# Row maximum in a spare PSUM column, read there by two one-column operations

## The chip, the cores and the metric

The kernel runs on one core of a Trainium2 chip, as one program from the load of the inputs to the last store. The metric is device time in microseconds. Inside the core five engines take their own instructions in order: PE (TensorE, matrix multiplication), DVE (VectorE), ACT (ScalarE), POOL (GpSimd) and SP (SyncE, which here only issues DMAs). PE writes into PSUM, eight banks of 512 fp32 columns by 128 partitions; DVE and ACT read and write PSUM and SBUF; POOL works on SBUF here.

## The reference, cut to what matters

Attention over 8 batches and 8 heads with a sequence of 576 and head dimension 64, where each row keeps only the scores within `tau` of its maximum, and then a mixture-of-experts layer over the 4608 resulting rows of 512:

```python
scores = scale * np.matmul(q, k.transpose(0, 1, 3, 2))     # scale = 1/8
thresh = np.max(scores, axis=-1, keepdims=True) - tau
scores = np.where(scores >= thresh, scores, -1000000000.0)
scores = scores - np.max(scores, axis=-1, keepdims=True)
attn = np.exp(scores)
attn = attn / (np.sum(attn, axis=-1, keepdims=True) + 1e-09)
attn_out = np.matmul(attn, v)
...
# MoE: rows with x @ w_skip > 0 go to the expert of the largest logit:
h = np.maximum(xc[mask] @ w1[e], 0.0)
y[mask] = gate_w[mask, None] * (h @ w2[e])
```

## The kernel before, in words

The attention works on 32 groups; a group `g` is two heads of one batch. Each group has nine items `i`: for each of four blocks of 128 query rows one item for either head, and a last item (`M`) that holds the 64 left-over rows of both heads. So there are 288 items, each a tile of 128 query rows by 576 keys. `plan_item` (L669) registers the steps of one item:

- `score` (L686, PE): two fp32 products of 288 columns, into two PSUM banks, of which columns 0 to 287 are used (`HS` is 288). A ring of three such pairs (`sps`, `SPB = 3`) is shared by the items; a pair is freed when the item's `mask` is done.
- `top` (L691, DVE): the maximum of the raw scores over both banks, into column 0 of the item's four columns of the SBUF tile `mx`.
- `small` (L695, DVE): one SCALAR_TENSOR_TENSOR on two columns, `mx[1:3] = cd[0:2] * mx[0] + cd[2:4]`. With the constant tile `cd` (1, -0.125, -8 tau, 0), built at the start (L400 to L404), it makes the threshold in column 1 and the bias of the exponential in column 2. Both of its tensor inputs, and its output, lie in SBUF.
- `expo` (L700, ACT): `exp(0.125 * score + bias)` from PSUM into the SBUF tile `p`.
- `mask` (L706, DVE): `(score >= threshold) * p`, from PSUM and SBUF into `p`.

After every second item, and after the ninth, `fph` (L510 on ACT, L512 on DVE) makes the f16 high part `pk` of `p`, `fpl` (L737, POOL) the f16 low part, and `turn` (L748 and L743, issued on SP) transposes them by DMA into `pt` or `ptm`. `plan_av` (L768) multiplies them with the values on PE (L788, L792); ACT takes the result out of PSUM, POOL scales it (L841, L854), and PE computes the router's logits (L923). The values themselves are split in two f16 parts by ACT and POOL (L645).

The order of all this on the engines is not written out. `Plan` (L138) is a list scheduler that runs when the program is built. Each operation has a key (item number minus an offset in `OFF`), dependencies, and an assumed duration per engine: 0.665 us for `top`, 0.13 us for `small`, 0.635 us for `expo`, 0.725 us for `mask`. `run` (L352) makes one schedule after another; each number in `SEEDS` perturbs the ranks of the one before it, and the last schedule is emitted. Where that schedule has PE idle, `emit` (L143) puts dummy matmuls of 256 columns (`fill`, L516, recorded as L518) into a bank that is free then: `int(FILL * idle / 0.115)` of them, with `FILL = 0.7`. The engines take their instructions in the emitted order; semaphores keep the data right whatever the real durations are.

The MoE layer follows after about 750 us of the profile. It is not touched by the change.

Of the kernel before, what the change touches and what calls it, by code (L numbers as in the profile page):

```python
# [12 lines left out]
F32 = mybir.dt.float32  # L13
# [4 lines left out]
AF = mybir.ActivationFunctionType  # L18
ALU = mybir.AluOpType
AX = mybir.AxisListType  # L20
# [4 lines left out]
P = 128  # L25
S = 576
# [8 lines left out]
HS = S // 2  # L35
# [15 lines left out]
STEP = 2 * NM + 1  # L51
NBK = 2 * NM + 1
SPB = 3
FILL = 0.7
SHB = 2
QB = 3
PFB = 4
# [21 lines left out]
SHARED = {"shp": 0, "gps": 0, "avp": 0, "sps": 2}  # L79
BANKS = 8  # L80
SEEDS = (
# [6 lines left out]
)  # L88
DLAT = 0.7
OFF = dict(  # L90
    ld=14.0, S=3.0, mx=2.4, sm=2.3, e=2.0, p=1.6, ph=0.6, phD=3.0, pl=0.4, tr=0.0, av=3.0, v=24.0, v0=20.0, ldv=-6.0, vsp=1.0, ld0=-30.0,
    init=6.0, row=2.0, rsp=0.5, L1=4.0, sc=0.0,
)

# [276 lines left out]
def attn_moe_kernel(ctx: ExitStack, tc: tile.TileContext, qk, vl, tau, wg, w1, w2, out):  # L371
    nc = tc.nc
# [24 lines left out]
    taue = cp.tile([P, 1], F32, name="taue")  # L397
    nc.scalar.activation(taue, cnt[:, 0:1], AF.Exp)
    nc.vector.tensor_scalar(taue, taub, 0.0, None, op0=ALU.max)
    cd = cp.tile([P, 4], F32, name="cd")  # L400
    nc.gpsimd.memset(cd[:, 0:1], 1.0)
    nc.gpsimd.memset(cd[:, 1:2], -0.125)
    nc.gpsimd.memset(cd[:, 3:4], 0.0)
    nc.vector.tensor_scalar(cd[:, 2:3], taue, -8.0, None, op0=ALU.mult)  # L404
    jt = cp.tile([P, P], F32R, name="jt")
    onesr = cp.tile([1, P], F32, name="onesr")

# [261 lines left out]
    def plan_item(g, i):  # L669
        n = STEP * g + i  # L670
        M = i == STEP - 1
        c, h = divmod(i, 2)
        ends = M or h == 1
        z = ("p", g, c)
        items = 1 if M else 2

        def two(t):
            return t.rearrange("p (a b) -> p a b", a=2)

        def score():  # L680
            T["S", g, i] = ps = sps()
            raw = T["raw", g]
            rs = slice(0, P) if M else slice(h * D, h * D + D)
            for j in range(2):
                ks = slice(QW + j * HS, QW + j * HS + HS)
                nc.tensor.matmul(ps[:, j, 0:HS], raw[rs, c * P : c * P + P], raw[rs, ks], start=True, stop=True)  # L686

        def top():
            if i == 0:
                T["mx", g] = ap_.tile([P, STEP, 4], F32, name="mx", tag="mx", bufs=3)  # L690
            nc.vector.tensor_reduce(T["mx", g][:, i, 0:1], T["S", g, i][:, :, 0:HS], AX.XY, ALU.max)  # L691

        def small():
            m = T["mx", g][:, i]
            nc.vector.scalar_tensor_tensor(m[:, 1:3], cd[:, 0:2], m[:, 0:1], cd[:, 2:4], op0=ALU.mult, op1=ALU.add)  # L695

        def expo():
            if h == 0:
                T[z] = ap_.tile([P, 2, S], F32, name="p", tag="p", bufs=PFB)
            nc.scalar.activation(  # L700
                two(T[z][:, h]), T["S", g, i][:, :, 0:HS], AF.Exp, bias=T["mx", g][:, i, 2:3], scale=0.125
            )

        def mask():
            e = two(T[z][:, h])
            nc.vector.scalar_tensor_tensor(  # L706
                e, T.pop(("S", g, i))[:, :, 0:HS], T["mx", g][:, i, 1:2], e, op0=ALU.is_ge, op1=ALU.mult
            )

        s = pl.op(n - OFF["S"], score, [T["q", g]] + ring.take("sps", SPB), {PE: 1.05 if M else 0.56})  # L710
        m = pl.op(n - OFF["mx"], top, [s] + (ring.take("mx", 3) if i == 0 else [T["m0", g]]), {DVE: 0.665})
        if i == 0:
            T["m0", g] = m
        m = pl.op(n - OFF["sm"], small, [m], {DVE: 0.13})
        e = pl.op(n - OFF["e"], expo, [m] + (ring.take("p", PFB) if h == 0 else T["es", g]), {ACT: 0.635})
        x = pl.op(n - OFF["p"], mask, [e], {DVE: 0.725})
        ring.free("sps", [x])
        T.setdefault(("Sop", g), []).append(s)
        T.setdefault(("es", g), []).append(e)
        T.setdefault(("ms", g), []).append(x)  # L720
        T.setdefault(("all", g), []).append(x)
        if M:
            ring.free("raw", T["Sop", g])
            ring.free("mx", T["all", g])
        if not ends:
            return
        ms, T["ms", g], T["es", g] = T["ms", g], [], []

        def fph(e):
            T["k", g, c] = ap_.tile([P, 2, 2 * S], F16, name="pk", tag="pk", bufs=KB)  # L730
            copy(e, T["k", g, c][:, 0:items, 0:S], T[z][:, 0:items])

        def fpl():
            k, p = T["k", g, c][:, 0:items], T.pop(z)[:, 0:items]
            for lo, w, at in ((0, NM * P, S + TL), (NM * P, TL, S)):
                ks = slice(lo, lo + w)
                nc.gpsimd.tensor_tensor(k[:, :, at : at + w], p[:, :, ks], k[:, :, ks], op=ALU.subtract)  # L737

        def turn():
            k = T.pop(("k", g, c))  # L740
            if M:
                T["pt", g, c] = PTM[g % MB]
                nc.sync.dma_start_transpose(T["pt", g, c][:, :, TL : TL + P], k[:, 0])  # L743
                return
            if c % 2 == 0:
                T["slot", g, c // 2] = wtile(F16, "pt", 2).rearrange("p (c a k q) -> p c a k q", c=2, a=2, q=P)
            T["pt", g, c] = pt = T["slot", g, c // 2][:, c % 2]
            nc.sync.dma_start_transpose(pt.rearrange("p a k q -> p (a k) q"), k.rearrange("p a b -> p (a b)"))  # L748

        w = items * S  # L750
        ph = pl.op(
            n - OFF["ph"],
            fph,
            ms + ring.take("pk", KB),
            {ACT: w / 1160 + 0.1, DVE: w / 1920 + 0.12},
            off={DVE: OFF["phD"]},
            port=BOTH,
        )
        lo = pl.op(n - OFF["pl"], fpl, [ph], {POOL: w * 0.00206 + 0.12})
        ring.free("p", [lo])  # L760
        q = ring.take("ptm", MB) if M else ring.take("wr", WRB) if c % 2 == 0 else [(T["tr", g, c - 1],)]
        t = T["tr", g, c] = pl.dma(n - OFF["tr"], turn, [ph, lo] + q, [0.35], 1.35 * items)
        ring.free("pk", [t])
        if M:
            for hd in range(2):
                plan_av(g, hd, n)
# [1141 lines left out]
```

## Time and profile before

| What | Value |
|---|---|
| median of 3 runs | 1059.12 us (1057.99 to 1062.39) |
| the profiled execution's own time | 1049.39 us |
| its span, first to last instruction | 1047.6 us |
| mean granted TensorE clock | 0.905 |
| busy share PE / DVE / ACT / POOL | 93% / 74% / 55% / 59% |
| attention, until the last `mask` | about 750 us of the span |

The profiled execution is 9.7 us shorter than the median of the three runs, and 1.8 us longer than its span. A busy share is the part of the span in which an engine was working on an instruction. PE's includes the dummy matmuls, and the ends of matmuls are modelled, so a busy PE need not be one at its peak. [...]

### The profile page before, as it was taken

What the parts mean: (1) busy time and instruction counts of PE and PEld (TensorE: products, weight loads), DVE (VectorE), ACT (ScalarE), POOL (GpSimd) and SP (SyncE); (2) the same over time, 40 slices, a digit from 0 to 9 for tenths busy, and PEclk for the clock granted to TensorE, in tenths of its full rate; (3) what the DMA queues carried; (4) which work ended last, traced back from release to release, by engine and by line L of the source; (5) the groups of instructions that cost most, each with busy time, mean ns of one, the idle gap of its engine ahead of it and who ended that gap; (6) DMA issues with size and microseconds to landing.
All of it is one profiled execution on the core that took longest, in us unless ns stands there. A gap on an engine that the chain in (4) does not pass through costs nothing. (4 is left out here: it accounts for less than half of the span.)

```text
span 1047.6 us, 21896 instructions
## 1 busy us (share of the span) xinstructions
PE 973.9 (93%) x8602; PEld 746.1 (71%) x8602; DVE 774.9 (74%) x1376; ACT 579.6 (55%) x872; POOL 617.8 (59%) x566
## 2 busy tenths in 40 slices
PE   7998999998989899899999999999988999999995
PEld 4666666766666676666656776666777989999994
DVE  7988698698679897968986788978645455557771
ACT  4766566666565676557656657645422434434450
POOL 4666575575466476656866576767715446444461
PEclk9999799699789898969987889977989999999998
DMA  6899697799579779958996689876943655344530
GB/s 177 170 194 151 119 234 155 131 208 202 106 160 177 177 143 229 182 105 165 181 207 140 152 202 167 156 156 116 191 152 124 214 181 160 129 164 175 191 126 17
DMA packets 371817, 169.79 MB, mean 162 GB/s; under 512 B 344270, under 2 KB 344270, under 8 KB 371712
## 3 DMA queue, kind: packets, MB, share of 16 engines
q1 hardware_dynamic: 367024, 158.72, 69.4%
q0 software_dynamic: 4544, 9.65, 2.9%
q8 instruction: 68, 1.11, 0.4%
q14 instruction: 37, 0.30, 0.1%
q10 hardware_dynamic: 144, 0.00, 0.0%
HBM read 69.46 MB, written 15.21 MB: 81 GB/s over the span
## 5 line engine op out<-in xcount | busy, mean ns | idle before, releaser
L737 POOL TENSOR_TENSOR pk<-p,pk 128x1024 f16<-128x1024 f32 (+1 forms) x320 | 366.8, 1170 | 230.6 <-issue 113.4
L686 PE MATMUL banks<-raw 64*128 64x288 f32 (+1 forms) x1152 | 377.4, 472 | 34.2 <-DVE p L706 32.1
L700 ACT ACTIVATE p<-banks,mx 128x576 f32<-128x576 f32 x288 | 210.2, 737 | 187.1 <-DVE mx L695 157.4
L691 DVE TENSOR_REDUCE mx<-banks 128x1 f32<-128x576 f32 x288 | 215.2, 751 | 113.6 <-PE banks L686 110.4
L686 PEld LDWEIGHTS banks<-raw 64*128 64x128 f32 (+1 forms) x1152 | 202.0, 207 | 115.0 <-DVE p L706 48.0
L706 DVE SCALAR_TENSOR_TENSOR p<-banks,mx,p 128x576 f32<-128x576 f32 x288 | 230.1, 807 | 8.6 <-ACT p L700 7.6
L510 ACT ACTIVATE pk<-p 128x1152 f16<-128x1152 f32 (+1 forms) x154 | 164.2, 1067 | 32.3 <-DVE p L706 21.0
L695 DVE SCALAR_TENSOR_TENSOR mx<-cd,mx 128x2 f32<-128x2 f32 x288 | 178.7, 625 | 2.4
L788 PEld LDWEIGHTS <-pt 128*128 128x128 f16 x2304 | 128.8, 104 | 26.7 <-issue 24.4
L518 PE MATMUL banks<-jt 128*128 128x256 f16 x874 | 138.3, 296 | 3.3 <-DVE p L706 2.2
L792 PE MATMUL banks<-Vl,pt 128*128 128x64 f16 x1280 | 139.2, 201 | 1.2 <-POOL Vl L645 1.2
L788 PE MATMUL banks<-Vh,pt 128*128 128x65 f16 x2304 | 139.8, 203 | 0.0
L518 PEld LDWEIGHTS <-jt 128*128 128x128 f16 x874 | 82.9, 105 | 68.7 <-issue 57.3
L792 PEld LDWEIGHTS <-pt 128*128 128x128 f16 x1280 | 122.8, 105 | 3.2 <-issue 0.5
L1542 POOL TENSOR_TENSOR wl<-wr,wh 128x1024 fp32r<-128x1024 f32 x28 | 72.4, 2603 | 35.3 <-ACT wh L1541 29.9
L1581 PE MATMUL hps<-xh,wl 128*128 128x256 f32 (+4 forms) x256 | 77.0, 301 | 0.0
L1581 PE MATMUL hps<-xh,wh 128*128 128x256 f32 (+4 forms) x248 | 76.4, 308 | 0.0
L1581 PE MATMUL hps<-xl,wh 128*128 128x256 f32 (+4 forms) x248 | 75.0, 302 | 0.0
L1582 ACT ACTIVATE HH<-hps 128x256 fp32r<-128x256 f32 (+4 forms) x64 | 27.0, 422 | 68.4 <-PE hps L1581 67.8
L1593 POOL DMA_INDIRECT out<-o,ids x21 | 21.1, 1006 | 72.0 <-DVE o L1592 28.9
L1541 ACT ACTIVATE wh<-wr 128x1024 fp32r<-128x1024 f32 x60 | 60.6, 1050 | 0.0
L1583 DVE SCALAR_TENSOR_TENSOR HH<-hps,HH 128x256 fp32r<-128x256 f32 (+4 forms) x64 | 31.1, 487 | 39.0 <-ACT HH L1582 38.9
(211 smaller groups left out, 1303.8 us busy)
## 6 DMA issues: line engine op xcount, KB each, us to landing
wr<-in_w SPq DMA_DIRECT2D x30, 1024.0 KB, 5.4
raw<-in_qk SPq DMA_DIRECT2D x32, 608.0 KB, 4.8
vraw<-in_vl SPq DMA_DIRECT2D x32, 320.0 KB, 4.2
out<-xb SPq DMA_DIRECT2D x32, 256.0 KB, 2.7
pt<-pk SPq DMA_TRANSPOSE x128, 5.2
rw<-in_w SPq DMA_DIRECT2D x2, 1024.0 KB, 6.4
out<-x SPq DMA_DIRECT2D x8, 128.0 KB, 2.8
lst<-rec,si POOLq DMA_INDIRECT x36, 3.9
```

The costliest lines, as they stand in the source:

```text
L510: nc.scalar.activation(dst, src, AF.Copy)
L518: nc.tensor.matmul(banks[:, n, 0 : 2 * P], x[:, 0:P], x[:, 0 : 2 * P], start=True, stop=True, skip_group_check=True)
L686: nc.tensor.matmul(ps[:, j, 0:HS], raw[rs, c * P : c * P + P], raw[rs, ks], start=True, stop=True)
L691: nc.vector.tensor_reduce(T["mx", g][:, i, 0:1], T["S", g, i][:, :, 0:HS], AX.XY, ALU.max)
L695: nc.vector.scalar_tensor_tensor(m[:, 1:3], cd[:, 0:2], m[:, 0:1], cd[:, 2:4], op0=ALU.mult, op1=ALU.add)
L700: nc.scalar.activation(two(T[z][:, h]), T["S", g, i][:, :, 0:HS], AF.Exp, bias=T["mx", g][:, i, 2:3], scale=0.125)
L706: nc.vector.scalar_tensor_tensor(e, T.pop(("S", g, i))[:, :, 0:HS], T["mx", g][:, i, 1:2], e, op0=ALU.is_ge, op1=ALU.mult)
L737: nc.gpsimd.tensor_tensor(k[:, :, at : at + w], p[:, :, ks], k[:, :, ks], op=ALU.subtract)
L788: nc.tensor.matmul(pv[:, c, :], x, Vh[:, vh, kt, :], start=(c + kt + i == 0), stop=False, skip_group_check=True)
L792: nc.tensor.matmul(pv[:, c, 0:D], x, Vl[:, vh, kt, :], start=False, stop=last, skip_group_check=True)
L1542: lo[q % 2].tensor_tensor(w[1][:, sl], rs, w[0][:, sl].bitcast(F32), op=ALU.subtract)
L1581: nc.tensor.matmul(hp_[:, 0:cap], w_, x, start=(i == 0), stop=(i == len(mm) - 1))
```

## The change

The maximum of a row no longer goes into SBUF. `top` writes it into the first unused column (288) of the item's own first PSUM bank. The combined operation `small` and its constant tile `cd` are gone. In their place, `bias` multiplies that PSUM column by -0.125 into column 1 of `mx`, and a new `small` adds `ntau8` (-8 tau, one SBUF column) to it, into column 0 of `mx`. Both are TENSOR_SCALAR operations of one column, both on DVE. `expo` depends on `bias` alone; `mask` depends on `small` and `expo`. The planner is told 0.13 us for each of the two, has a key offset for the new one (`th = 2.1`, between `sm = 2.3` and `e = 2.0`), gets another list of seeds (110 in place of 69), and `FILL` is 0.5 in place of 0.7.

```diff
-FILL = 0.7
+FILL = 0.5
...
 SEEDS = (
-    1000015, 1000126, 1000161, 1000217, 1000282, 1000349, 1000386, 1000531, 1000605, 1000703, 1000772, 1000861,
...
+    1000041, 1000097, 1000240, 1000273, 1000340, 1000508, 1000531, 1000880, 1000906, 1000984, 1001111, 1001210,
...
 OFF = dict(
-    ld=14.0, S=3.0, mx=2.4, sm=2.3, e=2.0, p=1.6, ph=0.6, phD=3.0, pl=0.4, tr=0.0, av=3.0, v=24.0, v0=20.0, ldv=-6.0, vsp=1.0, ld0=-30.0,
+    ld=14.0, S=3.0, mx=2.4, sm=2.3, th=2.1, e=2.0, p=1.6, ph=0.6, phD=3.0, pl=0.4, tr=0.0, av=3.0, v=24.0, v0=20.0, ldv=-6.0, vsp=1.0, ld0=-30.0,
...
-    cd = cp.tile([P, 4], F32, name="cd")
-    nc.gpsimd.memset(cd[:, 0:1], 1.0)
-    nc.gpsimd.memset(cd[:, 1:2], -0.125)
-    nc.gpsimd.memset(cd[:, 3:4], 0.0)
-    nc.vector.tensor_scalar(cd[:, 2:3], taue, -8.0, None, op0=ALU.mult)
+    ntau8 = cp.tile([P, 1], F32, name="ntau8")
+    nc.vector.tensor_scalar(ntau8, taue, -8.0, None, op0=ALU.mult)
...
-            nc.vector.tensor_reduce(T["mx", g][:, i, 0:1], T["S", g, i][:, :, 0:HS], AX.XY, ALU.max)
+            ps = T["S", g, i]
+            nc.vector.tensor_reduce(ps[:, 0, HS : HS + 1], ps[:, :, 0:HS], AX.XY, ALU.max)
+
+        def bias():
+            nc.vector.tensor_scalar(
+                T["mx", g][:, i, 1:2], T["S", g, i][:, 0, HS : HS + 1], -0.125, None, op0=ALU.mult
+            )

         def small():
-            m = T["mx", g][:, i]
-            nc.vector.scalar_tensor_tensor(m[:, 1:3], cd[:, 0:2], m[:, 0:1], cd[:, 2:4], op0=ALU.mult, op1=ALU.add)
+            nc.vector.tensor_scalar(T["mx", g][:, i, 0:1], T["S", g, i][:, 0, HS : HS + 1], ntau8, None, op0=ALU.add)
...
-                two(T[z][:, h]), T["S", g, i][:, :, 0:HS], AF.Exp, bias=T["mx", g][:, i, 2:3], scale=0.125
+                two(T[z][:, h]), T["S", g, i][:, :, 0:HS], AF.Exp, bias=T["mx", g][:, i, 1:2], scale=0.125
...
-                e, T.pop(("S", g, i))[:, :, 0:HS], T["mx", g][:, i, 1:2], e, op0=ALU.is_ge, op1=ALU.mult
+                e, T.pop(("S", g, i))[:, :, 0:HS], T["mx", g][:, i, 0:1], e, op0=ALU.is_ge, op1=ALU.mult
...
-        m = pl.op(n - OFF["sm"], small, [m], {DVE: 0.13})
-        e = pl.op(n - OFF["e"], expo, [m] + (ring.take("p", PFB) if h == 0 else T["es", g]), {ACT: 0.635})
-        x = pl.op(n - OFF["p"], mask, [e], {DVE: 0.725})
+        y = pl.op(n - OFF["sm"], bias, [m], {DVE: 0.13})
+        m = pl.op(n - OFF["th"], small, [m], {DVE: 0.13})
+        e = pl.op(n - OFF["e"], expo, [y] + (ring.take("p", PFB) if h == 0 else T["es", g]), {ACT: 0.635})
+        x = pl.op(n - OFF["p"], mask, [m, e], {DVE: 0.725})
```

## Rows read from the trace of the kernel before

**Rows 1.** Windows, the attention after its start: busy us (and instructions) by engine, clock, DMA.
```profile
50.00:752.00 702.00, 658.55 (x6375) 467.34 (x6372) 571.60 (x1034) 437.30 (x640) 453.77 (x419) 0.87 0.84 167
```

**Rows 2.** Windows, six attention stretches at granted clock 1.00 together: columns are named.
```profile
sum 306.20, PE 288.28 PEld 205.38 DVE 273.51 ACT 209.56 POOL 213.00; mean PE 48.05 PEld 34.23 DVE 45.59 ACT 34.93 POOL 35.50
```

**Rows 3.** The same six stretches, mask (L706) alone: length, busy us (count), clock, DMA.
```profile
59.20:100.00 40.80, 13.85 (x18) 1.00 0.99 184
117.20:154.60 37.40, 12.85 (x16) 1.00 1.03 220
205.90:250.10 44.20, 15.43 (x20) 1.00 0.99 208
349.30:403.70 54.40, 17.54 (x22) 1.00 0.79 159
468.80:523.30 54.50, 19.33 (x24) 1.00 0.85 168
608.70:683.60 74.90, 25.55 (x32) 1.00 0.87 174
```

**Rows 4.** The same six stretches: `small` (L695) alone, then dummy matmuls (L518) alone.
```profile
sum 306.20, DVE 78.19; mean DVE 13.03
```
```profile
sum 306.20, PE 53.92 PEld 33.38; mean PE 8.99 PEld 5.56
```

**Rows 5.** Windows, six attention stretches at granted clock 0.50 together.
```profile
sum 94.30, PE 93.55 PEld 61.73 DVE 55.05 ACT 46.09 POOL 52.94; mean PE 15.59 PEld 10.29 DVE 9.17 ACT 7.68 POOL 8.82
```

**Rows 6.** Those six slow-clock stretches, mask (L706) alone.
```profile
100.10:117.00 16.90, 3.65 (x5) 0.50 0.28 53
188.90:205.70 16.80, 4.29 (x6) 0.50 0.56 90
260.60:274.00 13.40, 3.17 (x4) 0.50 0.66 112
444.90:458.30 13.40, 4.66 (x6) 0.50 0.75 146
564.30:584.60 20.30, 4.28 (x6) 0.50 0.50 95
683.80:697.30 13.50, 3.24 (x4) 0.50 0.63 155
```

**Rows 7.** One line's instructions: count, duration ns min/median/max, first and last start.
```profile
L695 DVE SCALAR_TENSOR_TENSOR mx<-cd,mx x288: 187/308/3793, 10.4 to 748.4; 128x2 f32<-128x2 f32 x144
```
```profile
L706 DVE SCALAR_TENSOR_TENSOR p<-banks,mx,p x288: 743/808/820, 11.6 to 749.7; 128x576 f32<-128x576 f32 x144
```

**Rows 8.** Timeline of DVE: start us, us, engine, line, operation.
```profile
501.02 0.95 DVE L695 SCALAR_TENSOR_TENSOR mx<-cd,mx 128x2 f32<-128x2 f32 x1
...
513.93 1.35 DVE L695 SCALAR_TENSOR_TENSOR mx<-cd,mx 128x2 f32<-128x2 f32 x1
```

**Rows 9.** Timeline of POOL over the same stretch.
```profile
499.28 2.67 POOL L645 TENSOR_TENSOR Vl<-vraw,Vh 128x640 f16<-128x640 f32 x2
...
513.13 2.13 POOL L737 TENSOR_TENSOR pk<-p,pk 128x1024 f16<-128x1024 f32 x1 [1.05 <-issue]
```

**Rows 10.** The page's costliest groups: count, busy us, mean ns, idle us before and releaser.
```profile
L700 ACT ACTIVATE p<-banks,mx 128x576 f32<-128x576 f32 x288 | 210.2, 737 | 187.1 <-DVE mx L695 157.4
...
L695 DVE SCALAR_TENSOR_TENSOR mx<-cd,mx 128x2 f32<-128x2 f32 x288 | 178.7, 625 | 2.4
```

**Rows 11.** DVE's groups by form, small operations: two that read PSUM, one in SBUF.
```profile
L935 DVE COPY lg<-banks 128x64 f32<-128x64 f32 x8 | 1.7, 215 | 1.0 <-PE banks L923 1.0
...
L598 DVE TENSOR_SCALAR vmx<-vmx 1x1 f32<-1x1 f32 x8 | 1.1, 142 | 0.3
...
L994 DVE COPY lg<-banks 128x16 f32<-128x16 f32 x4 | 0.7, 168 | 5.7 <-PE banks L984 4.8 <-ACT p L700 0.9
```

**Rows 12.** Waits over the whole span: us in total, times, longest us.
```profile
DVE mx L691 <- PE banks L686: 110.4, 112, 3.6
...
DVE p L706 <- ACT p L700: 7.6, 14, 1.3
```

14 rows, old and new, of the table SEEDS are left out of this document.

## Prediction

> **What bounds the kernel now.** The change touches the attention alone, which fills the first 750 us of a span of 1047.6 us. I read the windows first. Over the attention after its start PE is busy 658.6 of 702 us, DVE 571.6, POOL 453.8, ACT 437.3, at a mean granted clock of 0.87 [rows 1]. That mean hides two regimes, so I cut it where the clock changes. In six long stretches at full clock (306.2 us) DVE is busy 89.3% and PE 94.1%, of which dummy matmuls are 53.9 us [rows 2, 4]. They hold 132 masks, one per item [rows 3], so an item takes 306.2 / 132 = 2.32 us, with 273.5 / 132 = 2.07 us of DVE work in it. In six stretches at 1.2 GHz (94.3 us) PE is busy 99%, DVE 58%, and with 31 masks an item takes 3.04 us [rows 5, 6]. So at full clock DVE sets the pace (PE close behind), at half clock PE does.
>
> How much is there of each? A mean of 0.87 between 1.0 and 0.5 makes 0.13 / 0.5 = 26% of 702 us, or 182 us, at half clock: 182 / 3.04 = 60 items. The other 228 of 288 run at full clock.
>
> Next, what DVE does. The combined operation on two columns takes 625 ns in the mean and 178.7 us in all [rows 10], but its durations run from 187 to 3793 ns, with a median of 308 [rows 7]. The timeline shows why. The one that starts at 513.93 lasts 1.35 us and ends at 515.28; POOL's TENSOR_TENSOR of 513.13 ends 2.13 us later, at 515.26. The one of 501.02 ends at 501.97, POOL's at 499.28 + 2.67 = 501.95 [rows 8, 9]. It stands on DVE until POOL's instruction is over. The mask, with one tensor from PSUM and one from SBUF, never does so: its 288 instructions take 743 to 820 ns, though POOL works beside many of them [rows 7]. ACT pays too: of its idle time before the exponential, 157.4 us end with this operation [rows 10].
>
> **The operation removed.** At full clock it costs 78.2 / 132 = 0.592 us per item [rows 3, 4].
>
> **The two operations added.** Neither has two tensors in SBUF, so like the mask they should not stand behind POOL. Small copies out of PSUM take 168 ns for 16 columns and 215 ns for 64 [rows 11]: 47 ns for 48 columns, about 1 ns each, so a single column is 168 - 15 = 153 ns. I take that: two cost 0.306 us. The lower bound is the single column in SBUF, 142 ns; the upper one 215 ns, as if the narrow one gained nothing [rows 11].
>
> [...]
>
> **Sum per item.** At full clock DVE's work falls from 2.07 by 0.592 - 0.306 = 0.286 us. If DVE keeps the busy share of 0.893 that it has now, an item becomes 0.286 / 0.893 = 0.320 us shorter, 2.00 us; over 228 items that is 73 us. With the bounds of the new operations it is 79 us (0.284 for two) or 41 us (0.43). At half clock PE is busy 99%, so I count nothing for those 60 items.
>
> **The maximum written to PSUM.** No DVE instruction writes PSUM in this trace. The gap between the slowest PSUM reader and the SBUF one, 215 - 142 = 73 ns [rows 11], bounds the change of the reduction both ways: 0.073 x 228 / 0.893 = 19 us. I take zero, because the reduction reads 576 PSUM columns in any case and writes one.
>
> **The threshold's new place.** It used to come with the bias and now has its own turn on DVE, planned ahead of the exponential (2.1 against 2.0) but not tied to it. It reads the bank that ACT reads for the exponential, so the program may have to order the two. Queued behind it on DVE stand other items' reductions and masks, and behind those PE's next scores, for which a mask frees the banks. The nearest row is the mask's wait for the exponential, 14 waits of 7.6 us in all [rows 12]; I take 8 us. The lower bound is zero; the upper one is the first rival below. Ahead of the exponential it costs ACT 0.15 us, covered by the 0.286 us by which the bias comes sooner.
>
> **Fewer dummy matmuls.** FILL 0.5 leaves 5 of 7 for the same planned idle. At full clock they stand where the planner sees PE idle; removing 2/7 of 53.9 us there frees nothing that DVE waits for. At half clock PE is the limit, and an item there is 1.04 us dearer than the 2.00 forecast. If the thinner filling lets the clock fall for half as many items again, 30 items cost 31 us; if it does not, PE's load in those stretches drops, at most by the same 2/7 of the fill share of full clock, 5%: 10 us of 182. I take zero. The constant tile, three small POOL writes and a narrower DVE one at the start, lies under the first loads: zero. The new seeds reorder every engine; their planner held the removed operation for 0.13 us, while it took 625 ns [rows 10], and now holds 0.26 us for what I put at 0.31, so the order is at least no worse informed. No term.
>
> **Total.** -73 + 8 = -65 us. The profiled execution would go from 1049.4 to 984 us. The median of the runs shown is 9.7 us above that execution, and I move it by the same amount: 1059.1 - 65 = 994 us.
>
> **Rivals.** *The threshold waits behind the exponential (slower).* If the two reads of one bank are kept apart and the threshold is emitted after the exponential has gone to ACT, DVE stands still until ACT is done, up to 0.737 us [rows 10]. In all items this is 0.737 x 228 / 0.893 = 188 us and undoes the gain by far; in half of them +94 - 73 = +21 us, 1080 us. It decides from an average stall of 0.286 us, 39% of the items. For it: nothing in the dependencies given to the planner ties these two. Against: the key puts the threshold first, and it is ready as soon as the bias is. [...] Chance 0.08.
>
> *PE becomes the bound (smaller gain).* At full clock PE without dummies is busy (288.3 - 53.9) / 132 = 1.78 us per item, and with 5/7 of the dummies 2.07 [rows 2 to 4]. At its present share of 0.941 that makes 2.20 us per item: 0.12 x 228 = 28 us, less the 8 us of waits, so 1039 us. For it: PE is busier than DVE now, and DVE waits 110 us for scores [rows 12]. Against: ends of matmuls are modelled, so busy PE has reserve, and dummies go where idle is planned. Chance 0.20.
>
> *The clock recovers (larger gain).* With DVE stalling less, PE pauses less, and the 60 items at half clock become fewer. Each that moves gives 1.04 us: half of them 31 us (963 us), all 62 us (932 us). For it: slow stretches alternate with fast ones all through the attention [rows 3, 6]. Against: there are fewer dummies. Chance 0.14.
>
> *No change*: as much lost to the first rival, or to PE, as is won: 0.06.
>
> **How the numbers follow.** The forecast itself, 964 to 1024 us, gets 0.52. Half a per cent (5.3 us) is about what a measurement of this kernel can tell from no change. Faster is 0.52 + 0.20 + 0.14 = 0.86, same 0.06, slower 0.08. The range goes from 940 us (most of the clock's case) to 1050 us (nearly all of PE's), leaving out about 0.04 below and 0.15 above; the bounds of the new operations, the reduction and the dummies lie inside it, singly and in pairs.
>
> **What the profile will show.** Right: both new operations near 0.15 us with no maxima beyond some 0.3; DVE near 1.79 us per item at full clock and an item near 2.0 us; the last mask near 685 us; the exponential's waits on DVE well below 157 us; about a third fewer dummies at an unchanged mean clock. Wrong: idle on DVE before the threshold released by ACT; one-column operations that still end with POOL's; PE's full-clock share above 97% with the item above 2.15 us; a reduction above 0.83 us; or a mean attention clock near 0.72: with 130 items at 3.04 us and 158 at 2.00 the attention takes as long as now (60 and 228), and 395 us of 711 at half clock make that mean.

## The result, and the profile after

| | median | range | ratio to before (95%) |
|---|---|---|---|
| before | 1060.72 us (4 runs) | 1057.99 to 1062.39 | |
| changed | 1025.85 us (4 runs) | 1022.98 to 1036.66 | 0.969 (0.962 to 0.977) |

The change makes the kernel 3.1% faster. The direction was forecast, and the time lies in the range (940 to 1050 us), but the gain is 35 us (33 by the ratio) where 65 were forecast. The profiled execution of the changed kernel took 1027.18 us, with a span of 1025.4 us and a mean granted clock of 0.879 (0.905 before). The profiled execution of the kernel before took 1049.39 us, 11.3 us less than its median here, so the two profiles differ by only 22 us. Executions over 1.5% above a kernel's fastest are left out of all medians and ratios below (in e13 four of seven, 994.1 to 1010.5 us beside 978.2 to 982.7).

First the operations themselves: DVE's groups by line (count, busy us, mean ns, idle before and who ended it), then single lines (duration ns min/median/max). In the changed kernel the score is L687, the maximum L693, `bias` L696, `small` (the threshold) L701, the exponential L706 and the mask L712.

```profile
L712 DVE SCALAR_TENSOR_TENSOR p<-banks,mx,p 128x576 f32<-128x576 f32 x288 | 231.1, 810 | 11.5 <-ACT p L706 8.8 <-ACT vmx L620 1.1
L693 DVE TENSOR_REDUCE banks<-banks 128x1 f32<-128x576 f32 x288 | 218.4, 761 | 163.5 <-PE banks L687 160.6 <-issue 2.1
L701 DVE TENSOR_SCALAR mx<-banks,ntau 128x1 f32<-128x1 f32 x288 | 58.7, 209 | 21.8 <-ACT p L706 20.5
...
L696 DVE TENSOR_SCALAR mx<-banks 128x1 f32<-128x1 f32 x288 | 42.6, 151 | 0.6
```
```profile
L701 DVE TENSOR_SCALAR mx<-banks,ntau x288: 153/209/220, 10.3 to 730.9; 128x1 f32<-128x1 f32 x144
```
```profile
L696 DVE TENSOR_SCALAR mx<-banks x288: 93/150/160, 9.5 to 730.8; 128x1 f32<-128x1 f32 x144
```

The combined operation cost 178.7 us [rows 10] with durations up to 3793 ns [rows 7]; the two that replace it cost 101.3 us and none exceeds 220 ns. Neither of them stands behind POOL, although 170 of the one and 178 of the other start while a TENSOR_TENSOR of POOL has over 0.1 us still to run. Before, 104 of the 288 combined operations took over 0.5 us, and every one of them ended within 60 ns of the end of a TENSOR_TENSOR on POOL. The longest stood through four of these that followed each other without a gap (the kernel before, DVE and then POOL; 439.62 + 3.79 = 443.41, 438.43 + 4.97 = 443.40):

```profile
439.62 3.79 DVE L695 SCALAR_TENSOR_TENSOR mx<-cd,mx 128x2 f32<-128x2 f32 x1
...
438.43 4.97 POOL L737 TENSOR_TENSOR pk<-p,pk 128x1024 f16<-128x1024 f32 x4
```

That part went as forecast, and DVE's busy time in the whole span fell by 94 us (774.9 to 681.2). Its idle time before a reduction, waiting for scores from PE, rose from 110 us [rows 12] to 161 us. About half of what DVE saved stands there as another wait.

The waits of the changed kernel (us in total, times, longest) that answer to [rows 10, 12]:

```profile
DVE banks L693 <- PE banks L687: 160.6, 154, 5.2
ACT p L706 <- DVE mx L696: 80.7, 72, 3.3
...
ACT p L706 <- DVE mx L701: 30.1, 28, 3.0
...
DVE mx L701 <- ACT p L706: 20.5, 35, 3.4
...
DVE p L712 <- ACT p L706: 8.8, 12, 1.7
```

The exponential waits 80.7 us for the bias (157.4 us before) and 30.1 us for the threshold, in 28 waits. The fourth line is the wait that the first rival named, the threshold behind an exponential: 35 times, 20.5 us.

Then the two regimes, now over all of the attention in place of six stretches each. The windows cover every stretch at one clock up to the last mask, a granted share of 1.00 or 0.50 in each. No run shows a frequency: the prediction's stretches at 1.2 GHz are those at 0.50 [rows 5]. Of each answer the sum line is shown, for all engines and for the mask alone. The mask's busy time divided by its mean is the number of items (it gives 285 of the 288 in every kernel, since busy time counts overlaps once, so all times per item are alike 1% too long). Before, 20 stretches at full clock and 19 at half:

```profile
sum 565.18, PE 517.77 PEld 367.39 DVE 498.72 ACT 375.16 POOL 371.07; mean PE 25.89 PEld 18.37 DVE 24.94 ACT 18.76 POOL 18.55
...
sum 565.18, DVE 182.87; mean DVE 9.14
...
sum 177.53, PE 176.12 PEld 123.08 DVE 111.76 ACT 90.94 POOL 104.52; mean PE 9.27 PEld 6.48 DVE 5.88 ACT 4.79 POOL 5.50
...
sum 177.53, DVE 47.20; mean DVE 2.48
```

The changed kernel, 19 and 18 stretches:

```profile
sum 502.48, PE 470.30 PEld 329.06 DVE 396.75 ACT 351.88 POOL 345.03; mean PE 24.75 PEld 17.32 DVE 20.88 ACT 18.52 POOL 18.16
...
sum 502.48, DVE 171.74; mean DVE 9.04
...
sum 225.27, PE 222.63 PEld 158.30 DVE 124.18 ACT 114.27 POOL 128.73; mean PE 12.37 PEld 8.79 DVE 6.90 ACT 6.35 POOL 7.15
...
sum 225.27, DVE 59.35; mean DVE 3.30
```

| | full clock: us per item | DVE share | PE share | half clock: us, items |
|---|---|---|---|---|
| before | 565.2 / 226.6 = 2.49 | 0.88 | 0.92 | 178, 58 |
| changed | 502.5 / 212.0 = 2.37 | 0.79 | 0.94 | 225, 73 |

At full clock an item became 0.12 us shorter, not 0.32. And 48 us more of the attention run at half clock in these two executions. But the one profiled before was unusual: its mean clock of 0.905 lies above those of all 44 executions of that kernel beside the experiments (0.869 to 0.902, median 0.890), while the changed kernel's four have 0.875 to 0.884. With these two levels, 1.00 and 0.50, a mean clock c over a span T makes 2 x (1 - c) x T at half clock. As an estimate, that is about 233 us of a usual execution before (0.890 of 1060 us) and 242 us of the changed kernel (0.8815 of 1023 us). So most of the 48 us come from which execution was profiled. What the changed kernel lacks is not clock that it lost but clock that it did not gain, as e2 below will show. Three parts of the change could account for the small gain: the operations, the thinner filling, and the new order. The experiments take them apart.

### The profile page after: what moved, and what is told of

It reads as the page before. It is cut to its first block, busy times and chain, and to the rows that moved or that the text cites. A ratio compares the mean times of both kernels' runs of the same rounds, so it can differ in the third digit from the quotient of the medians.

```text
span 1025.4 us, 21731 instructions
## 1 busy us (share of the span) xinstructions
PE 966.4 (94%) x8350; PEld 737.4 (72%) x8350; DVE 681.2 (66%) x1666; ACT 580.2 (57%) x870; POOL 616.3 (60%) x563
## 5 line engine op out<-in xcount | busy, mean ns | idle before, releaser
L687 PE MATMUL banks<-raw 64*128 64x288 f32 (+1 forms) x1152 | 391.6, 483 | 25.1 <-DVE p L712 19.9
L693 DVE TENSOR_REDUCE banks<-banks 128x1 f32<-128x576 f32 x288 | 218.4, 761 | 163.5 <-PE banks L687 160.6
L687 PEld LDWEIGHTS banks<-raw 64*128 64x128 f32 (+1 forms) x1152 | 210.4, 211 | 108.4 <-DVE p L712 35.3
L706 ACT ACTIVATE p<-banks,mx 128x576 f32<-128x576 f32 x288 | 209.4, 737 | 130.0 <-DVE mx L696 80.7
L712 DVE SCALAR_TENSOR_TENSOR p<-banks,mx,p 128x576 f32<-128x576 f32 x288 | 231.1, 810 | 11.5 <-ACT p L706 8.8
L511 ACT ACTIVATE pk<-p 128x1152 f16<-128x1152 f32 (+1 forms) x152 | 161.7, 1064 | 63.5 <-DVE p L712 28.6
L795 PEld LDWEIGHTS <-pt 128*128 128x128 f16 x2304 | 139.0, 108 | 30.3 <-issue 27.3
L795 PE MATMUL banks<-Vh,pt 128*128 128x65 f16 x2304 | 150.0, 209 | 1.2 <-issue 1.2
L799 PE MATMUL banks<-Vl,pt 128*128 128x64 f16 x1280 | 149.6, 207 | 0.2 <-issue 0.2
L799 PEld LDWEIGHTS <-pt 128*128 128x128 f16 x1280 | 129.2, 109 | 3.7 <-issue 1.5
L519 PE MATMUL banks<-jt 128*128 128x256 f16 x622 | 104.7, 297 | 0.7 <-DVE p L712 0.7
L519 PEld LDWEIGHTS <-jt 128*128 128x128 f16 x622 | 57.3, 105 | 58.7 <-issue 51.4
L701 DVE TENSOR_SCALAR mx<-banks,ntau 128x1 f32<-128x1 f32 x288 | 58.7, 209 | 21.8 <-ACT p L706 20.5
L1548 ACT ACTIVATE wh<-wr 128x1024 fp32r<-128x1024 f32 x60 | 60.6, 1050 | 0.0
L1549 DVE TENSOR_TENSOR wl<-wr,wh 128x1024 fp32r<-128x1024 f32 x32 | 52.5, 1656 | 8.4 <-ACT wh L1548 7.9
```

Source lines behind the costliest of these rows:

```text
L511: nc.scalar.activation(dst, src, AF.Copy)
L519: nc.tensor.matmul(banks[:, n, 0 : 2 * P], x[:, 0:P], x[:, 0 : 2 * P], start=True, stop=True, skip_group_check=True)
L693: nc.vector.tensor_reduce(ps[:, 0, HS : HS + 1], ps[:, :, 0:HS], AX.XY, ALU.max)
L706: nc.scalar.activation(two(T[z][:, h]), T["S", g, i][:, :, 0:HS], AF.Exp, bias=T["mx", g][:, i, 1:2], scale=0.125)
L712: nc.vector.scalar_tensor_tensor(e, T.pop(("S", g, i))[:, :, 0:HS], T["mx", g][:, i, 0:1], e, op0=ALU.is_ge, op1=ALU.mult)
L795: nc.tensor.matmul(pv[:, c, :], x, Vh[:, vh, kt, :], start=(c + kt + i == 0), stop=False, skip_group_check=True)
```

## Experiments

Every run is compared with the kernel before on its own chip. Runs of one group (e1 to e4, e5 to e8, e9 to e12, e13 to e15) share a chip; across groups the ratios are compared, and a difference in us is a difference of ratios times 1060.7.

| run | what | median us | ratio (95%) |
|---|---|---|---|
| e1 | changed, FILL 0.7 | 1010.4 | 0.950 (0.946 to 0.955) |
| e2 | old order and FILL, new operations | 987.8 | 0.929 (0.924 to 0.934) |
| e3 | changed order and FILL, old operation | 1093.4 | 1.027 (1.022 to 1.032) |
| e4 | changed, threshold right behind bias | 1015.3 | 0.955 (0.950 to 0.959) |
| e5 | e2 with FILL 0.5 | 1000.8 | 0.945 (0.939 to 0.951) |
| e6 | e2 with the maximum in SBUF | 993.3 | 0.939 (0.932 to 0.945) |
| e7 | e2 with FILL 1.0 | 1004.3 | 0.948 (0.942 to 0.954) |
| e8 | e4 with FILL 0.7 | 1013.2 | 0.954 (0.946 to 0.961) |
| e9 | e2 and one more DVE operation per item | 994.2 | 0.942 (0.936 to 0.948) |
| e10 | e2 with less work on PE | 974.2 | 0.925 (0.919 to 0.930) |
| e11 | before with less work on PE | 1060.3 | 1.010 (1.004 to 1.017) |
| e12 | e1, FILL 1.0 from item 192 | 1024.9 | 0.974 (0.968 to 0.980) |
| e13 | e2, order of 48 seeds | 980.3 | 0.923 (0.916 to 0.930) |
| e14 | e8, order of 80 seeds | 998.0 | 0.939 (0.933 to 0.944) |
| e15 | e2, FILL 1.0 up to item 96 | 991.2 | 0.933 (0.929 to 0.938) |

### The operations alone: e2 and e3

e2, in the kernel before:

```diff
-            nc.vector.tensor_reduce(T["mx", g][:, i, 0:1], T["S", g, i][:, :, 0:HS], AX.XY, ALU.max)
+            ps = T["S", g, i]
+            nc.vector.tensor_reduce(ps[:, 0, HS : HS + 1], ps[:, :, 0:HS], AX.XY, ALU.max)
...
-            nc.vector.scalar_tensor_tensor(m[:, 1:3], cd[:, 0:2], m[:, 0:1], cd[:, 2:4], op0=ALU.mult, op1=ALU.add)
+            nc.vector.tensor_scalar(m[:, 2:3], top_, -0.125, None, op0=ALU.mult)
+            nc.vector.tensor_scalar(m[:, 1:2], top_, cd[:, 2:3], None, op0=ALU.add)
```

e3 is the reverse, in the changed kernel: the old operation at the place of `bias`, nothing at that of `small`.

> The kernel before with only the operations exchanged: maximum into the PSUM column, and two one-column operations at the place of the combined one, in the old order, with FILL 0.7. The prediction's own step (DVE keeps its busy share of 0.893 at full clock) gives 65 us less, about 995 us. Theory A (clock and filling) agrees with that, since the filling stays: 990 to 1005 us. Theory B (PE becomes the bound): 20 to 35 us less, 1025 to 1040 us. Theory C (the new seeds lost the gain): 995 us or less, below the changed kernel by 30 us.

> The changed kernel, its order and its FILL of 0.5, with the old combined operation on SBUF at the place of the bias and the maximum in SBUF. If the exchange of operations is worth 65 us in any order, 1090 us, which would say that new order and FILL cost some 30 us. Theory B: the exchange is worth 20 to 35 us, so 1045 to 1060 us. The operation should again end with POOL's instructions, with a mean near 0.6 us.

The exchange is worth 7.1% in the old order (75 us) and 5.8% in the new one (0.969 against 1.027, 61 us). So the operations do about what was forecast for them, in both orders. In e3 the old operation stands behind POOL as before (98 of the 288 take over 0.5 us, and each ends within 60 ns of the end of a TENSOR_TENSOR there), and the kernel is 2.7% slower than the one before: new order and thinner filling by themselves are a loss.

```profile
L700 DVE SCALAR_TENSOR_TENSOR mx<-cd,mx x288: 152/223/4285, 9.9 to 795.2; 128x2 f32<-128x2 f32 x144
```

The same windows of e2, 13 stretches at full clock and 12 at half:

```profile
sum 574.97, PE 550.21 PEld 395.05 DVE 459.77 ACT 408.64 POOL 411.45; mean PE 42.32 PEld 30.39 DVE 35.37 ACT 31.43 POOL 31.65
...
sum 574.97, DVE 202.80; mean DVE 15.60
...
sum 112.64, PE 112.45 PEld 76.59 DVE 58.68 ACT 57.45 POOL 63.82; mean PE 9.37 PEld 6.38 DVE 4.89 ACT 4.79 POOL 5.32
...
sum 112.64, DVE 27.25; mean DVE 2.27
```

An item at full clock takes 575.0 / 251.3 = 2.29 us, with DVE busy 80% and PE 96%. The 75 us are near the 73 forecast for the operations, but by another route. 227 items at 0.21 us less give 47 us; 25 items that moved from half to full clock give 18 us; the 34 that stayed are 0.3 us dearer, 10 us back. That makes the 55 us by which the attention shrank between these two profiles. Over usual executions more of it is clock: e2's runs have mean clocks of 0.925 to 0.938, the kernel before 0.890. In the new order the exchange brings clock too, from 0.847 to 0.860 in e3's runs to 0.875 to 0.884.

### The filling: e1, e5 and e7

```diff
-FILL = 0.5
+FILL = 0.7
```

> The changed kernel with FILL 0.7 again; nothing else differs, so the order of all other work is the same. Theory A (thinner filling lets the clock fall): the half-clock time of the attention, 225 us in the changed kernel against 177 us before, comes back by at least half, and the time falls by 15 to 30 us, to 996 to 1011 us. Theory B (PE is simply full; dummies only take its time): about 250 dummies of 0.11 us more, time the same or up to 15 us longer, 1026 to 1041 us. Theory C (the order from the new seeds is what lost the gain): no change beyond 5 us.

> The old order with the two new operations (988 us with FILL 0.7), with FILL 0.5. Theory A (thinner filling costs clock): 10 to 25 us longer, 998 to 1013 us, and the half-clock time of the attention, 113 us with FILL 0.7, above 160 us. If the filling matters only in the order of the new seeds: 983 to 993 us, and the whole rest of the distance to the changed kernel (1026 us) is the order.

> The old order with the two new operations, with FILL 1.0 in place of 0.7: some 380 dummies more. Theory A: the 113 us at half clock shrink below 80 us and the time falls by 5 to 15 us, to 973 to 983 us. Theory B (PE is full at full clock, 96% busy): dummies delay scores, an item at full clock goes above 2.3 us and the time rises to 990 to 1005 us.

Going from 0.7 to 0.5 costs 20 us in the new order (0.950 to 0.969) and 17 us in the old one (0.929 to 0.945). The mean clocks of all runs agree: 0.916 to 0.931 in e1 against 0.875 to 0.884, and 0.925 to 0.938 in e2 against 0.890 to 0.908 in e5. In the new order the profile shows where: with 926 dummies in place of 622 the attention is at half clock for 133 us, not 225.

```profile
sum 133.12, PE 129.93 PEld 92.05 DVE 71.88 ACT 68.24 POOL 75.45; mean PE 9.28 PEld 6.57 DVE 5.13 ACT 4.87 POOL 5.39
```

But clock is not yet time. With the threshold right behind the bias (e4 and e8, below) the same step in the new order lifts the clock as much, from 0.878 to 0.894 over e4's runs to 0.918 to 0.934 over e8's, and is worth nothing (0.955 and 0.954).

More is not better either: at 1.0 (e7) the half-clock time goes down to 96 us, yet an item at full clock takes 613.4 / (208.96 / 0.806) = 2.37 us, 0.08 us more over 259 items, and the kernel is 20 us slower than at 0.7. Filling trades clock against PE's own time.

```profile
sum 613.44, PE 600.14 PEld 439.99 DVE 471.71 ACT 422.02 POOL 416.55; mean PE 60.01 PEld 44.00 DVE 47.17 ACT 42.20 POOL 41.66
...
sum 613.44, DVE 208.96; mean DVE 20.90
...
sum 95.56, PE 94.81 PEld 63.70 DVE 47.27 ACT 44.33 POOL 58.77; mean PE 10.53 PEld 7.08 DVE 5.25 ACT 4.93 POOL 6.53
```

### What sets the pace at full clock: e9, e10 and e11

The first line is e9's, against e2; the rest is the edit of e10 (against e2) and e11 (against the kernel before), which leaves out part of the output's precision.

```diff
+            nc.vector.tensor_scalar(m[:, 3:4], top_, cd[:, 2:3], None, op0=ALU.add)
...
-                    if i == 0:
+                    if i == 0 and last:
                         nc.tensor.matmul(pv[:, c, 0:D], x, Vl[:, vh, kt, :], start=False, stop=last, skip_group_check=True)
```

> The old order with the two new operations and FILL 0.7 (988 us), with a third one-column operation behind them, a copy of the threshold's that nobody reads: about 0.21 us on DVE per item, 0.13 us net of the overlap between neighbours. If DVE sets the pace at full clock, as the prediction had it (share 0.893): 0.13 / 0.893 for each of 256 items, 37 us more, 1025 us. If PE sets it: less than 12 us more, 988 to 1000 us.

> The old order with the two new operations and FILL 0.7, without the products of the values' low parts but the last of each head; this leaves out a part of the output's precision, and 1536 of 1600 small matmuls of 0.03 us at full clock, 46 us of PE or 0.16 us per item. If PE sets the pace: 25 to 45 us less, 943 to 963 us, unless the clock falls more often with the work that is gone. If DVE does: 980 to 990 us.

> The kernel before without the same low-part products (the same part of the output's precision is left out). If DVE set the pace at full clock before the change and PE does after it, the same cut is worth less here than in the kernel with the new operations: 0 to 20 us, 1042 to 1062 us. If PE set the pace in both: 30 to 45 us, 1017 to 1032 us.

(`last` holds once per head; so one low-part product of 25 is left, 1536 of 1600 go.) The extra DVE operation costs about 13 us, not 37: slightly over PE's 12, far from DVE's. Its windows at full clock, and the sum at half clock:

```profile
sum 569.06, PE 543.86 PEld 391.26 DVE 478.49 ACT 408.38 POOL 403.58; mean PE 38.85 PEld 27.95 DVE 34.18 ACT 29.17 POOL 28.83
...
sum 569.06, DVE 199.64; mean DVE 14.26
...
sum 126.28, PE 125.50 PEld 84.65 DVE 71.51 ACT 58.64 POOL 71.30; mean PE 9.65 PEld 6.51 DVE 5.50 ACT 4.51 POOL 5.48
```

DVE's share rises from 0.80 to 0.84 and the item goes from 2.29 to 569.1 / (199.64 / 0.808) = 2.30 us: DVE fills gaps that it had. The half-clock time rose from 113 to 126 us. Less work on PE gave 5 us by the ratios (0.925 against 0.929, within their intervals), far less than the 25 to 45 expected. At full clock PE's work per item fell by 0.10 us (550.2 / 251.3 = 2.19 to 485.8 / 232.3 = 2.09), not by the 0.16 expected, and the item from 2.29 to 516.3 / (187.97 / 0.809) = 2.22 us, 16 us over these 232 items. But the half-clock time rose from 113 to 164 us and took most of that back.

```profile
sum 516.30, PE 485.83 PEld 338.10 DVE 423.86 ACT 387.22 POOL 382.71; mean PE 28.58 PEld 19.89 DVE 24.93 ACT 22.78 POOL 22.51
...
sum 516.30, DVE 187.97; mean DVE 11.06
...
sum 163.83, PE 160.89 PEld 106.59 DVE 94.10 ACT 79.62 POOL 92.82; mean PE 10.06 PEld 6.66 DVE 5.88 ACT 4.98 POOL 5.80
```

In the kernel before the same cut leaves an item at full clock where it was (496.1 / (160.63 / 0.808) = 2.50 us against 2.49, DVE 90% busy) and only adds half-clock time, 256 us in place of 178. The clocks of all runs agree (0.851 to 0.868, against 0.872 to 0.902 before on that chip). The kernel is 1.0% slower (0.4 to 1.7%) for having less to do; neither of the two expected ranges, 0 to 20 and 30 to 45 us less, allowed for a loss.

```profile
sum 496.11, PE 441.15 PEld 302.46 DVE 445.20 ACT 338.25 POOL 329.31; mean PE 15.76 PEld 10.80 DVE 15.90 ACT 12.08 POOL 11.76
...
sum 496.11, DVE 160.63; mean DVE 5.74
...
sum 256.00, PE 253.37 PEld 168.32 DVE 166.06 ACT 127.80 POOL 146.42; mean PE 9.38 PEld 6.23 DVE 6.15 ACT 4.73 POOL 5.42
```

So DVE did set the pace before, as the prediction read it; with the operation's stalls gone it no longer does, and PE counts for part of it. What sets the rest was not tested. A candidate is the loop through the three pairs of PSUM banks, in which a maximum waits for a score and a score for the mask that frees its banks: its depth was not varied.

### PSUM or only one SBUF input: e6

Against e2:

```diff
-            ps = T["S", g, i]
-            nc.vector.tensor_reduce(ps[:, 0, HS : HS + 1], ps[:, :, 0:HS], AX.XY, ALU.max)
+            nc.vector.tensor_reduce(T["mx", g][:, i, 0:1], T["S", g, i][:, :, 0:HS], AX.XY, ALU.max)
...
-            m, top_ = T["mx", g][:, i], T["S", g, i][:, 0, HS : HS + 1]
+            m = T["mx", g][:, i]
+            top_ = m[:, 0:1]
```

> The old order, FILL 0.7, two one-column operations as in the changed kernel, but the maximum stays in SBUF and both read it there. Theory D (what cost the time was the second SBUF input of the combined operation, and PSUM is not needed): the operations take about 0.14 and 0.2 us and never end with POOL's; 983 to 993 us, or some us less than with the PSUM column, because the threshold no longer shares a bank with the exponential. Rival (a one-column TENSOR_SCALAR within SBUF also stands behind POOL): a maximum above 1 us in these two lines, and 1030 to 1100 us, as two operations would each wait.

```profile
L696 DVE TENSOR_SCALAR mx<-mx x288: 96/144/155, 10.3 to 692.3; 128x1 f32<-128x1 f32 x144
```
```profile
L697 DVE TENSOR_SCALAR mx<-mx,cd x288: 191/203/206, 10.4 to 692.4; 128x1 f32<-128x1 f32 x144
```

In SBUF the two operations take 144 and 203 ns and never stand behind POOL, although 185 and 186 of them start while a TENSOR_TENSOR runs there. The kernel runs at 0.939, its interval overlapping e2's 0.929. So PSUM is not needed for the gain: what went with the old operation is its second SBUF tensor (`cd` is read here as a scalar operand, one value per partition). Its second column went too, and one operation of two columns with a single tensor was not tried; but the mask, the same kind of instruction over 576 columns with one tensor in SBUF, never stood behind POOL (743 to 820 ns [rows 7]). The spare PSUM column adds about one per cent, which these intervals, from two chips, do not tell from nothing.

### The threshold's place and the order: e4, e8, e12 to e15

e4 and e8 issue both operations at the place of `bias`; e12 and e15 change the filling of a range of keys; e13 and e14 stop the search early.

```diff
+            nc.vector.tensor_scalar(T["mx", g][:, i, 0:1], T["S", g, i][:, 0, HS : HS + 1], ntau8, None, op0=ALU.add)
         def small():
-            nc.vector.tensor_scalar(T["mx", g][:, i, 0:1], T["S", g, i][:, 0, HS : HS + 1], ntau8, None, op0=ALU.add)
+            pass
...
-            for _ in range(int(FILL * o.idle[0] / 0.115)):
+            for _ in range(int((1.0 if 189 <= o.key < 290 else FILL) * o.idle[0] / 0.115)):
...
-    pl.run(SEEDS)
+    pl.run(SEEDS[0:80])
```

> The changed kernel with the threshold issued right behind the bias, in one place of DVE's order, and nothing at its own place. No threshold waits for an exponential any more (35 waits of 20.5 us in the changed kernel), but each exponential that reads the same bank may wait 0.2 us longer. If the threshold's waits are what ate the gain: 15 to 20 us less, 1006 to 1011 us. If they are covered by DVE's waits for PE: within 5 us of 1026 us.

> The changed kernel's order with the threshold issued right behind the bias (1015 us with FILL 0.5), with FILL 0.7. If filling (15 us measured in this order) and the threshold's place (11 us) add up: 1000 us. What is then left to the old order with the same operations and filling (988 us) is the new order itself, about 12 us. If they overlap: 1005 to 1011 us.

Moving the threshold is worth 1.5% at FILL 0.5 (0.969 to 0.955, intervals that just do not touch) and nothing at 0.7 (0.950 and 0.954, intervals that overlap). So its waits cost between nothing and 15 us; that is not settled better. With the same operations at the same places and the same filling, the new order (e8, 0.954) is 26 us behind the old one (e2, 0.929); at FILL 0.5 the same two orders are only 10 us apart (e4, 0.955, and e5, 0.945, intervals that touch).

Against e1, which has the threshold apart, e2 is better in both parts: an item of e1 at full clock takes 576.0 / (198.90 / 0.809) = 2.34 us, not 2.29, and 133 us are at half clock, not 113.

```profile
sum 575.99, PE 555.35 PEld 396.44 DVE 449.91 ACT 398.22 POOL 398.28; mean PE 37.02 PEld 26.43 DVE 29.99 ACT 26.55 POOL 26.55
...
sum 575.99, DVE 198.90; mean DVE 13.26
```

Windows of e1 and then e2, the first 96 items and the last two times 48 (busy us by engine, then clock, DMA share, GB/s):

```profile
0.00:225.00 225.00, 217.26 (x2145) 153.65 (x2146) 173.51 (x463) 156.64 (x229) 152.20 (x170) 0.98 0.95 192
...
461.60:595.00 133.40, 127.59 (x1103) 89.06 (x1101) 86.49 (x235) 76.98 (x111) 78.18 (x73) 0.77 0.84 168
595.00:715.30 120.30, 117.35 (x1244) 84.94 (x1242) 88.87 (x255) 74.64 (x107) 88.65 (x83) 0.90 0.85 159
```
```profile
0.00:238.50 238.50, 227.55 (x2141) 159.32 (x2141) 171.40 (x454) 159.66 (x232) 150.79 (x172) 0.89 0.90 180
...
472.20:587.20 115.00, 109.92 (x1096) 78.38 (x1094) 85.45 (x226) 75.91 (x111) 84.41 (x80) 0.93 0.93 191
587.20:693.00 105.80, 102.92 (x1141) 75.25 (x1140) 88.75 (x258) 73.32 (x107) 87.12 (x81) 1.00 0.92 178
```

The new order is 13.5 us ahead after 96 items, with the higher clock, and loses 33 us over the last 96, with the lower one. That suggested the clock as the whole cause, and filling as the cure:

> The changed kernel with FILL 0.7, and 1.0 from item 192 on, where that order had clocks of 0.77 and 0.90 (the old order with the same operations 0.93 and 1.00) and lost 33 us to it: 133.4 and 120.3 us for 48 items each against 115.0 and 105.8. If the new order's loss there is the clock: the clock of those stretches rises above 0.88 and the time falls by 8 to 20 us from the 1010 us with 0.7 throughout, to 990 to 1002 us. If its order stalls there whatever the clock: 1005 to 1020 us.

```profile
463.60:589.00 125.40, 120.13 (x1156) 85.30 (x1155) 86.60 (x237) 76.87 (x111) 79.58 (x74) 0.87 0.87 182
589.00:720.60 131.60, 127.82 (x1326) 94.37 (x1325) 89.47 (x255) 74.76 (x107) 87.33 (x81) 0.90 0.76 142
```

That theory fell as a cure. The first of the two stretches gained 8 us with its clock (0.77 to 0.87), the last lost 11 us at an unchanged 0.90, and by the ratios the whole is 2.4% slower than e1. The profile explains little of that: it is of the fastest of e12's executions (1014.9 us, clock 0.938, where the median is 1024.9 us), and its attention is only 5 us longer than e1's. e15 did the same where the old order's clock is low:

> The old order with the two new operations (988 us), FILL 0.7 but 1.0 for the first 96 items, where its clock was 0.89 (0.91 to 1.00 later). If denser filling can buy clock where the clock is low: 238 us for these items becomes 228 us and the total 978 to 983 us, the fastest here. If dummies cost as much as the clock returns, as FILL 1.0 throughout did: 988 to 998 us.

It neither gained nor lost (0.933 against 0.929, intervals that overlap). The last two ask whether orders simply scatter:

> The old order's search stopped at 48 of its 69 seeds, with the two new operations and FILL 0.7: a third order from the same planner. If an order's time is not what the planner ranks by (PE's clock, and waits that it does not know), it lands within 25 us of the full list's 988 us on either side, say 975 to 1012 us, and the 22 us between old and new order are of the size by which orders differ anyway. If the old list's search was worth its time on the chip: above 1012 us.

> The new order's search stopped at 80 of its 110 seeds, threshold behind the bias, FILL 0.7 (with all 110: 1013 us). If orders of the new planner costs are worse as such (two operations at 0.13 us, threshold apart): 1005 to 1025 us. If they scatter: anywhere between 985 and 1030 us, and below 1000 us would say that the new list is one unlucky order.

The new list's do: stopped at 80 seeds it gives 0.939 where all 110 give 0.954. The planner's last thirty steps cost the chip 16 us. The old list at 48 seeds gives 0.923, from three executions, where 69 give 0.929; these intervals overlap. The two old-planner orders are nonetheless ahead of both new-planner ones, though e14's interval touches e2's. With two orders each, whether the new planner costs are worse as such stays open, and so does what in the new order costs the time.

## Why the prediction was right in its direction and wrong in its size

The steps that failed in the sum are two terms set at nothing, the filling and the order. Together with the threshold's place, for which the sum had 8 us, they cost 42 us, the distance from e2 to the changed kernel (0.929, 0.969).

**Right.** What bounds the kernel, and why the operation was slow: DVE at full clock (e11), an operation that stands until POOL's ends, where the two of one column that replace it in e6 take 206 ns at most. The bias, 153 ns forecast and 151 measured. The reduction into PSUM, taken as no change: 761 ns where it took 751 into SBUF. The exchange of operations by itself: 73 us forecast, 75 measured (e2), though that agreement is partly luck, as the first failed step shows. The first rival's wait exists, 35 times for 20.5 us where I took 8, too little to turn the sign; that it comes from the shared bank was not shown. By e4 (against the changed kernel) and e8 (against e1) the threshold's place is worth between nothing and 15 us.

**Sized too low.** The threshold, 153 ns forecast, takes 209, nearly the upper bound of 215. Its extra 56 ns are its SBUF scalar operand: in e6, with all in SBUF, the same pair differs by as much (144 and 203). That the one adds and the other multiplies is not it: at the start of the changed kernel, an addition and a multiplication of a constant over eight columns take 162 (L477) and 164 ns (L479). Two other TENSOR_SCALARs of one column there, once each, have two constants (L480) or one constant and one scalar operand from SBUF (L481), and differ by 68 ns:

```profile
L481 DVE TENSOR_SCALAR tokp<-tokp,iop 128x1 f32<-128x1 f32 x1 | 0.2, 213 | 0.0
...
L480 DVE TENSOR_SCALAR tokp<-iop 128x1 f32<-128x1 f32 x1 | 0.1, 145 | 0.0
```

**Failed, and made good by luck in e2: "If DVE keeps the busy share of 0.893 that it has now."** Its share fell to 0.79 in the changed kernel and 0.80 in e2, and an item at full clock got 0.12 and 0.21 us shorter, not 0.32. In e2 that is 47 us in place of 73, and the clock, for which the sum had nothing, made up the rest. The second rival had the share: PE's was already above DVE's. It gave 2.20 us per item from a base of 2.32, 0.12 less, which is what the changed kernel did; but e2 did better, and by e10 PE sets only part of the pace. The base itself was low: the six stretches ran at 2.32 us per item, all 20 at 2.49.

**Failed: "Fewer dummy matmuls ... I take zero."** In the changed kernel as it stands it costs 20 us (e1), in the old order 17 (e5), inside the bound of 31 us that stood beside the zero. I priced both ends and took the middle. With the threshold right behind the bias it costs 1 us (e4 and e8).

**Failed: "The new seeds reorder every engine ... No term."** The order that they produce costs 26 us against the old one at FILL 0.7 (e8 and e2) and 10 us at 0.5 (e4 and e5), with the same operations at the same places. A better informed planner was taken for a better order.

**The sum.** From the changed kernel to e2 there are three ways through the runs: filling 20 us, then order and place together 22 (e1); place 15, filling 1, order 26 (e4, e8); place 15, order 10, filling 17 (e4, e5). Each must make 42 us, because its ends are the same two runs, so that 75 - 42 = 33 us (0.031 x 1060.7) proves no single price. What is shown is that the three together cost 42 us and that each one's share depends on the other two.

The third rival (the clock recovers) came true in e2, 178 to 113 us at half clock. In the changed kernel it did not: in usual executions about as much of the time is at half clock as before (estimated above, 242 and 233 us).

The best version here that computes the same keeps the old order and FILL 0.7 and takes only the new operations: e2, 988 us on the chip where the kernel before takes 1064, with e13 not distinguishable from it.

## What to carry to other kernels

A small operation whose durations scatter from 0.2 to 4 us need not be costly by its work: look at what ends when it ends, and ask whether other operands, with the same arithmetic, avoid it. A saving on the engine that sets the pace may be worth its full size only up to the next limit, so put the second engine's share beside the sum before dividing by the first one's. And when a change comes with a new schedule and a retuned constant, run each as a change of its own before believing a price for it: here they gave back more than half of what the operation won.

## What the runs showed of the hardware

- A DVE operation of two columns with two tensors in SBUF waited for TENSOR_TENSORs of POOL to end: before, 104 of 288 took over 0.5 us and ended within 60 ns of the end of one, the longest (3.8 us) stood through four that followed each other without a gap; in e3 the longest took 4.3 us. Operations of one column with at most one tensor in SBUF, also beside a scalar operand from SBUF, did not in any of 288 instructions (at most 220 ns in the changed kernel, 206 ns in e6).
- One column out of PSUM or SBUF costs DVE nearly the same in the median: 148 (e2) against 144 ns (e6), and 207 against 203 ns with a scalar operand from SBUF, 59 ns more in either.
- A reduction that writes its one column into PSUM takes 761 ns (changed kernel), 751 into SBUF (before).
- Taking 1536 small matmuls off PE made the kernel before 1.0% slower (e11): the time at granted clock 0.50 rose from 178 to 256 us in the profiled executions.
- More granted clock is not always less time: from e4 to e8 the mean clock rose (0.878 to 0.894 over e4's runs, 0.918 to 0.934 over e8's), and the ratio stayed (0.955, 0.954).
